# Reordering the start and the seventh pair of a fused routed-attention and SwiGLU kernel

## The chip, the cores and the metric

The kernel runs on one core of a Trainium2 chip. The metric is the device time of one execution in microseconds (us). The kernel before takes 367.86 us (median of 3 runs, 367.55 to 368.01).

## The reference

```python
# routed attention: B=4, H=8, S=768, D=64, 16 centroids for each head
q_assign = argmax(q_n @ c_n.T);  k_assign = argmax(k_n @ c_n.T)      # normalised rows
scores = scale * q @ k.T, -1e9 where q_assign != k_assign
attn = softmax(scores) @ v
# feed-forward on x = attn, as (3072, 512); d_ff = 1536
xn = x / rms(x) * rms_g
out = (silu(xn @ w_gate) * (xn @ w_val)) @ w_out
```

## The kernel before

Heads go in pairs; there are 16 pairs, `pi` 0 to 15, called the first to the sixteenth here. Each pair is prepared: q and k are transposed on TensorE (four pieces, T0 to T3), copied out of PSUM, multiplied with the centroids (`sp`), and the argmax becomes a one-hot matrix, which 16 extra rows of the score operand (`aug`) receive by DMA. So the routing mask comes out of the score matmul itself.

```python
on_dve = (g % 2 == 0 if pi == 0 else g > 1 if pi == 1 else pi < 6 or g % 2)
if on_dve:
    nc.vector.tensor_copy(dst, tp)          # VectorE (DVE)
else:
    nc.scalar.copy(dst, tp)                 # ScalarE (ACT)
# ... cut
def place():                                # one-hot rows into aug, four DMAs of 24 KB
    # ... cut
    eng = nc.sync
    if pi == 0:
        eng = nc.gpsimd if side else nc.scalar
    eng.dma_start(out=aug[st][a][D:KA, side, :].rearrange("c (r n) -> c r n", r=2),
                  in_=ohT[r:r + 2 * NC, :])
```

A main loop of 288 steps does one score chunk of 512 columns for each step (nine steps are one head, a slot). Up to step 96 three chunks share a wide PSUM tile (`scw`) and one exponential. From step 96 on, pieces of the feed-forward (gp, vp, dp) are woven in. All else is hung on steps with `at(step, fn)`; functions of one step run in the order in which they were hung there.

```python
# ... cut: first pair prepared, T0 to T3 and casts of the second
keep_warm(8)                                # dummy matmuls
for i in (SP, ARG1, ARG2, PLACE, CASTV):
    p1[i]()
first.close()
late["wide"] = wide.enter_context(tc.tile_pool(name="ps_wide", bufs=2, space=PSUM))
load_pair(3)
at(4, lambda: load_pair(4))
# ... cut
for pi in range(2, B * NP):
    base = 2 * NCH * (pi - 2) + {2: 4, 3: 1, 6: 6}.get(pi, 0)
    steps = (0, 2, 4, 6, 7, 9, 10, 12, 12, 10) if pi < 7 else (0, 1, 3, 4, 5, 8, 9, 11, 11, 9)
    for fn, step in zip(prep_parts(pi), steps):     # T0 T1 T2 T3 CAST SP ARG1 ARG2 PLACE CASTV
        at(base + step, fn)
# ... cut: weight loads
for b in range(B):                          # RMS work of the four batches
    steps = (9, 9, 10, 10, 11, 12, 13, 15, 17, 19, 20, 22, 24, 26)
    for fn, step in zip(rms_parts(b), steps):
        at(H * NCH * (b + 1) + step, fn)
```

The RMS part of a batch is: sums of squares on ScalarE and VectorE, their inverse root on GpSimd (`ir`), three normalised tiles `xn` on VectorE, and a transposing DMA (`xnT`) that feeds gp and vp; all this twice.

The softmax here doesn't subtract the row's maximum and nothing guards it: scores larger than these inputs give would overflow.

## Time and profile before

| | before |
|---|---|
| median time | 367.86 us |
| span of the profiled run | 364.7 us |
| TensorE (PE) busy | 340.2 us, 93% |
| VectorE, ScalarE busy | 222.0 and 228.0 us |
| mean granted clock | 0.985 |
| first wide score (scw) starts | 16.30 us |
| first feed-forward matmul (gp) starts | 78.81 us |

How to read the views: a page cuts the span into 40 equal slices (numbered from 0 here), and a digit is the busy share of a slice in tenths; the PEclk row is the clock that TensorE was granted, in tenths of full speed. "L287" is line 287 of the kernel, and `out<-in` names what an instruction writes and reads.

TensorE is the bound from about 91 us on. The prediction shows the lines for that, for the waits before it, and for the stretch of half clock at 67 to 77 us.

### The profile page before, as it was taken

To read this page: it belongs to the slowest core of one execution; us is meant where nothing else is said; L and a number is where in the kernel's file an instruction comes from. 1 tells how busy PE (TensorE), PEld (TensorE's weight loads), DVE (VectorE), ACT (ScalarE), POOL (GpSimd) and SP (SyncE) were. 2 spreads that over 40 slices of the span, in tenths; PEclk is the share of its full clock that TensorE was granted. 3 is DMA by queue.
4 is the path that set the end of the run, shared out by engine and by line. 5 is a ranking of instruction groups with operands and counts; after the bars stand their busy time and mean duration, and the time that the engine had idled before them with its cause. 6 is when DMAs were issued, how large, how long until landed. Compare 5 with 4: busy or idle time off the path is not lost.

```text
span 364.7 us, 7453 instructions
## 1 busy us (share of the span) xinstructions
PE 340.2 (93%) x2930; PEld 204.5 (56%) x2930; DVE 222.0 (61%) x443; ACT 228.0 (63%) x395; POOL 85.8 (24%) x119
## 2 busy tenths in 40 slices
PE   7878997688999999999999999999999979999996
PEld 4446665355666665656565665656666635555542
DVE  4766663667666648695665658695544586555540
ACT  3487888656787776867676767767777343232321
POOL 2554551762414041321204041320000011000000
PEclk9999999679999999999999999999999999999999
DMA  7449499289992310735051001431000013100012
GB/s 242 160 136 291 158 217 209 62 112 113 281 221 103 113 58 25 192 75 168 0 164 38 12 31 36 49 78 38 29 2 31 30 51 86 38 31 29 31 58 86
DMA packets 38242, 35.38 MB, mean 97 GB/s; under 512 B 15072, under 2 KB 35008, under 8 KB 38208
## 3 DMA queue, kind: packets, MB, share of 16 engines
q1 hardware_dynamic: 32080, 30.06, 27.8%
q0 software_dynamic: 5888, 4.77, 9.4%
q8 instruction: 23, 0.38, 0.4%
q10 hardware_dynamic: 240, 0.08, 0.1%
q14 instruction: 11, 0.09, 0.1%
HBM read 28.61 MB, written 6.29 MB: 96 GB/s over the span
## 4 chain that ended last, share of the span: by engine, by line
PE 75%; DVE 13%; ACT 5%; DMA 3%; issue 2%; POOL 1%; ACTq 0%; DVEq 0%
PE dp L401 15%; PE vp L372 15%; PE gp L372 15%; PE sc L287 9%; PE acc L301 7%; PE tp L193 6%; PE scw L287 4%; DVE xn L343 3%; PE sp L229 3%; DMA q_in<-in_q_dram 3%; ACT pT L290 2%; DVE gvT L387 1%; ACT jk L326 1%; DVE oh L244 1%; DVE qk L197 1%
## 5 line engine op out<-in xcount | busy, mean ns | idle before, releaser
L290 ACT ACTIVATE pT<-sc 128x512 bf16<-128x512 f32 x192 | 113.3, 597 | 54.7 <-PE sc L287 53.6
L381 DVE SCALAR_TENSOR_TENSOR uu<-th,gp 128x384 f32<-128x384 f32 x96 | 53.0, 553 | 72.9 <-ACT th L377 72.6
L372 PE MATMUL vp<-xnT,wv 128*128 128x384 bf16 x384 | 78.1, 325 | 2.6 <-DVE gvT L387 2.3
L372 PE MATMUL gp<-xnT,wg 128*128 128x384 bf16 x384 | 78.1, 325 | 1.2 <-DVE uu L381 1.0
L401 PE MATMUL dp<-wo,gvT 128*128 128x512 bf16 x288 | 76.0, 378 | 2.9 <-ACT ob L407 1.5
L377 ACT ACTIVATE th<-gp 128x384 f32<-128x384 f32 x96 | 47.1, 491 | 47.9 <-PE gp L372 44.9
L216 POOL CAST aug<-qk 64x768 bf16<-64x768 f32 x60 | 52.1, 868 | 103.8 <-DVE qk L197 100.6
L301 PEld LDWEIGHTS <-pT 128*128 128x128 bf16 x1152 | 58.5, 98 | 29.1 <-issue 3.4
L287 PE MATMUL sc<-aug 80*128 80x512 bf16 (+1 forms) x256 | 72.9, 326 | 0.0
L301 PE MATMUL acc<-vbf,pT 128*128 128x65 bf16 x1152 | 64.3, 195 | 0.2 <-DVE x L311 0.2
L387 DVE TENSOR_TENSOR gvT<-uu,vp 128x384 bf16<-128x384 f32 x96 | 52.6, 548 | 6.5 <-PE vp L372 1.4
L372 PEld LDWEIGHTS <-wg 128*128 128x128 bf16 x384 | 37.2, 97 | 30.2 <-issue 2.3
L290 ACT ACTIVATE pT<-scw 128x1536 bf16<-128x1536 f32 x32 | 45.0, 1452 | 14.4 <-PE scw L287 14.2
L372 PEld LDWEIGHTS <-wv 128*128 128x128 bf16 x384 | 37.0, 97 | 22.3 <-issue 4.2
L401 PEld LDWEIGHTS <-gvT 128*128 128x128 bf16 x288 | 27.9, 97 | 29.1 <-issue 4.4
L287 PEld LDWEIGHTS <-aug 80*128 80x128 bf16 x384 | 34.0, 98 | 17.7 <-POOL vbf L221 4.4
L197 DVE COPY qk<-tp 128x384 f32<-128x384 f32 x40 | 22.1, 554 | 25.6 <-PE tp L193 25.6
L287 PE MATMUL scw<-aug 80*128 80x512 bf16 (+1 forms) x128 | 27.2, 337 | 1.9 <-DVE tr L236 0.7
L334 POOL TENSOR_SCALAR ir<-ss 128x3 f32<-128x3 f32 x8 | 1.6, 196 | 97.8 <-ACT jk L326 97.8
L343 DVE SCALAR_TENSOR_TENSOR xn<-x,ir,g_b 128x512 bf16<-128x512 bf16 x24 | 20.5, 863 | 5.5 <-POOL ir L335 5.4
L193 PE MATMUL tp<-ident_f,k_in 128*128 128x128 f32 x96 | 17.7, 296 | 5.3 <-ACT qk L199 4.3
L193 PE MATMUL tp<-ident_f,q_in 128*128 128x128 f32 x96 | 17.8, 298 | 3.0 <-DMA q_in<-in_q_dram 2.0
(54 smaller groups left out, 204.2 us busy)
## 6 DMA issues: line engine op xcount, KB each, us to landing
q_in<-in_q_dram SPq DMA_DIRECT2D x16, 384.0 KB, 4.7
k_in<-in_k_dram SPq DMA_DIRECT2D x16, 384.0 KB, 5.1
v_in<-in_v_dram SPq DMA_DIRECT2D x16, 384.0 KB, 5.7
out_dram<-ob SPq DMA_DIRECT2D x24, 256.0 KB, 2.0
wg<-in_moe_w_gate_dram POOLq DMA_DIRECT2D x4, 384.0 KB, 5.4
wv<-in_moe_w_val_dram POOLq DMA_DIRECT2D x4, 384.0 KB, 6.7
wo<-in_moe_w_out_dram POOLq DMA_DIRECT2D x4, 384.0 KB, 7.2
aug<-ohT SPq DMA_DIRECT2D x60, 24.0 KB, 1.9
```

The costliest lines, as they stand in the source:

```text
L193: nc.tensor.transpose(tp[:, i * P:(i + 1) * P], src[:, a, i * P:(i + 1) * P], ident_f)
L197: nc.vector.tensor_copy(dst, tp)
L216: nc.gpsimd.tensor_copy(aug[st][a][0:D, :, par * HS:(par + 1) * HS], qk32[0][par * D:(par + 1) * D, 2 * a:2 * a + 2, :])
L287: nc.tensor.matmul(sc[:, o:o + n], lhsT=ag[:, 1, kc * P:(kc + 1) * P], rhs=ag[:, 0, qo:qo + n], start=True, stop=True)
L290: nc.scalar.activation(pts[slot][:, j * CH:(j + nch) * CH], sc[:, :nch * CH], ACT.Exp, scale=scale)
L301: nc.tensor.matmul(acc[:, TORD[g], :], lhsT=pts[slot][:, kc * S + g * P:kc * S + (g + 1) * P], rhs=vb[:, a, TORD[kc], :], start=(kc == 0), ...
L343: nc.vector.scalar_tensor_tensor(st["xn"][:, tl, :], x_t[b][:, t, :], st["ir"][:, tl:tl + 1], g_b, op0=ALU.mult, op1=ALU.mult)
L372: nc.tensor.matmul(pt[:, :HS], lhsT=w[:, dc, fc * P:(fc + 1) * P], rhs=xnT[b, m][:, :, dc, :], start=(dc == 0), stop=(dc == DC - 1))
L377: nc.scalar.activation(th, pt[:, :HS], ACT.Tanh, scale=0.5)
L381: nc.vector.scalar_tensor_tensor(uu, th, 1.0, pt[:, :HS], op0=ALU.add, op1=ALU.mult)
L387: nc.vector.tensor_tensor(gvT[half][:, fc, :], uu, pt[:, :HS], op=ALU.mult)
L401: nc.tensor.matmul(dp, lhsT=gvT[hf][:, f, tl * P:(tl + 1) * P], rhs=wo[:, f, :], start=(f == 0), stop=(f == FC - 1))
```

## The change

Its intent: let the first scores start before the second pair's argmax, bring the fourth pair's inputs early, and prepare the seventh pair with VectorE copies and ahead of the RMS work, so that its copies don't stand behind exponentials.

```diff
-            on_dve = (g % 2 == 0 if pi == 0 else g > 1 if pi == 1 else pi < 6 or g % 2)
+            on_dve = (g % 2 == 0 if pi == 0 else g > 0 if pi == 1 else pi < 7 or g % 2)
     keep_warm(8)
-    for i in (SP, ARG1, ARG2, PLACE, CASTV):
-        p1[i]()
     first.close()
     late["wide"] = wide.enter_context(tc.tile_pool(name="ps_wide", bufs=2, space=PSUM))
     load_pair(3)
+    for i, step in ((SP, 0), (ARG1, 0), (ARG2, 1), (PLACE, 1), (CASTV, 1)):
+        at(step, p1[i])
     ... cut
+    for b in range(B):
+        steps = (9, 9, 10, 10, 11, 12, 13, 15, 17, 19, 20, 22, 24, 26)
+        for fn, step in zip(rms_parts(b), steps):
+            at(H * NCH * (b + 1) + step, fn)
     for pi in range(2, B * NP):
-        base = 2 * NCH * (pi - 2) + {2: 4, 3: 1, 6: 6}.get(pi, 0)
+        base = 2 * NCH * (pi - 2) + {2: 3, 3: 1, 7: 4}.get(pi, 0)
     ... cut: the same RMS loop removed from behind the weight loads
```

More of the change, by code (lines that the diff above doesn't have):

```diff
@@ L468 @@
         at(step, lambda i=i: w_load(i))
-    for b in range(B):
-        steps = (9, 9, 10, 10, 11, 12, 13, 15, 17, 19, 20, 22, 24, 26)
-        for fn, step in zip(rms_parts(b), steps):
-            at(H * NCH * (b + 1) + step, fn)
     def extras(step):
```

## The prediction

> **What bounds the kernel now.** I read the page first, to see whether one engine carries the span.
>
> ```profile
> span 364.7 us, 7453 instructions
> PE 340.2 (93%) x2930; PEld 204.5 (56%) x2930; DVE 222.0 (61%) x443; ACT 228.0 (63%) x395; POOL 85.8 (24%) x119
> PE   7878997688999999999999999999999979999996
> PEclk9999999679999999999999999999999999999999
> ```
>
> TensorE is the bound over most of the span: from slice 10 on (after about 91 us) it is nearly always at 9. The change touches only what lies before that, so no more can be won than the idle or slow time of TensorE in the first 90 us. The PEclk row has a hole in slices 7 and 8 (64 to 82 us), where TensorE also has its lowest digits. So I took the timeline of TensorE next; its columns are start, duration, group, and in brackets the idle time before it with its releaser.
>
> ```profile
> 16.30 1.46 PE L287 MATMUL scw<-aug 80*128 80x512 bf16 x8 [0.71 <-DVE tr L236]
> 27.85 0.52 PE L193 MATMUL tp<-ident_f,q_in 128*128 128x128 f32 x3 [1.29 <-DMA q_in<-in_q_dram]
> 60.99 0.55 PE L193 MATMUL tp<-ident_f,k_in 128*128 128x128 f32 x3 [1.52 <-ACT qk L199]
> 64.77 0.55 PE L193 MATMUL tp<-ident_f,k_in 128*128 128x128 f32 x3 [0.95 <-ACT qk L199]
> 68.45 1.50 PE L229 MATMUL sp<-qk,cbd 128*32 128x384 f32 x8 [1.93 <-DVE qk L197]
> 73.60 0.90 PE L193 MATMUL tp<-ident_f,k_in 128*128 128x128 f32 x3 [1.27 <-ACT qk L199]
> 78.81 0.81 PE L372 MATMUL gp<-xnT,wg 128*128 128x384 bf16 x4
> ```
>
> The reader sees the three places at which the change aims: the first scores (16.30) wait for the second pair's argmax to free PSUM; the fourth pair's transposes (27.85) wait for a load; and the seventh pair's transposes and assignment wait for PSUM copies that stand on ScalarE behind exponentials, or on VectorE behind the RMS normalization. From 68.45 the eight assignment pieces take 1.50 us instead of the 0.85 they take elsewhere. The clock explains it; I asked for stretches of 3.41 us (length, PE busy, granted clock, DMA share, GB/s):
>
> ```profile
> 12.47:15.88 3.41, 2.53 (x12) 1.00 0.20 58
> 26.12:29.53 3.41, 2.12 (x26) 1.00 0.97 347
> 63.67:67.08 3.41, 1.91 (x31) 1.00 0.31 105
> 67.08:70.49 3.41, 2.04 (x15) 0.50 0.01 2
> 70.49:73.91 3.42, 2.15 (x9) 0.50 0.64 116
> 73.91:77.32 3.41, 3.41 (x28) 0.50 1.19 133
> 77.32:80.73 3.41, 2.84 (x36) 1.00 0.81 126
> ```
>
> A stretch with 1.91 us of busy time is followed by half clock; stretches with 2.12 and more are not; full clock returns only after a stretch that was full.
>
> How much is lost: steps 78 to 96 of the program (57.93 to 78.59 us) last 20.66 us with 14.35 us of PE; a comparable 18 steps before (45.99 to 55.45) last 9.46 us. So the hole is 11.2 us wide, 3% of the span; part is real work (transposes of two pairs instead of one, RMS), and 3.8 us of it (half of the 7.6 busy at half clock) is slow clock.
>
> [...] The 0.95 and 1.52 us above are that: a 0.5 us copy behind a 1.45 us exponential. [...] one-hot pieces behind loads on SyncE's queue landed after 5.8 us (median), those on other queues after 2.0. [...] Here xn takes 1.3 us beside the GpSimd casts and 0.746 in the median.
>
> **The change part by part.**
>
> *Start, second pair.* Removed: the 0.71 us wait for the argmax before the first scores, and one ScalarE copy. The first scores then need only the first pair's one-hot pieces, whose weight load could go at 15.5 us in the profile; so 0.5 to 0.8 us earlier. But the assignment (0.8 us), which filled TensorE at 13.1 to 15.6, moves behind the first scores. TensorE is then idle from 13.2 (end of the dummy matmuls) to about 15.7. The argmax chain on VectorE (0.58+0.55+0.6+0.25+0.58, about 2.7 with gaps) starts at about 17.2 instead of 15.67, and ends at 20.0 instead of 19.1. The third pair's copies stand behind it, one PSUM buffer serves its transposes, and the instruction order now has two of these before the third wide score, where there was one. So that score moves from 18.70 to about 21.1, and ScalarE idles. By my sum the fourth exponential comes at 23.3 instead of 22.11: a loss of 1.2 us.
>
> *Fourth pair's loads.* They leave SyncE's queue at about 8 to 11 us instead of 21.89 to 23.0, ahead of the one-hot pieces, so the 1.29 us wait at 26.55 goes. With the loss above, the scores at 28.40 come at about 27.75: 0.4 to 0.65 us won, if the clock holds. If it does not (idle 2.5 us in a window leaves 0.9 busy of 3.41, far under the 1.91 that throttled), half clock from about 16 us for two or three windows doubles some 4 us of TensorE work; about half hides in its 25 to 30% idle there. That costs 2 us (estimate). I give the throttle 7 in 10. Expected sum: 0.5 - 0.7 x 2 = 0.9 us lost.
>
> *Seventh pair.* It starts six steps earlier and copies all four pieces on VectorE (0.56 each; 2 x 0.5 leave ScalarE). Its steps then repeat the pattern of the sixth pair, which cost 9.46 us per 18 steps. That removes the waits 1.52, 0.95 and 1.93 and what follows from them. But the next stage begins with gp (78.81), the first reader of the transposed RMS output[...]. So I follow that chain. By the sixth pair's pattern the exponential of step 81 ends 7.54 us after step 72: 55.45 + 7.54 = 63.0 (before: 63.74). Two Squares end at 64.3, GpSimd's ir at 65.5 (1.17; before 66.61). On VectorE two xn take 2.0, then the seventh pair's one-hot work, which now stands between them (1.5), then the third xn (0.75): 69.8, before 70.4. And SyncE now issues the four one-hot DMAs (2.5 us) ahead of the DMA transpose: from about 69.0 to 71.5. The transpose was issued at 70.42 before and landed 6.0 us later; now 71.5 + 4.6 to 6.0 = 76.1 to 77.5. So gp gains only 78.81 - 76.8 = 2.0 us, though the work before it may be done at 72.
>
> TensorE idles 4 to 5 us there, and the throttle is nearly certain: one to two windows at half clock in a stage which it bounds cost 1.7 to 3.4, say 2.4 x 0.9 = 2.2 us. Against it: VectorE is ahead by then, and 1.36 us of TensorE idle at 82 to 88 goes; the eighth pair's last two transposes move into this stage (+0.7). Sum: -2.0 + 2.2 - 1.4 + 0.7 = -0.5 us.
>
> Steady state beyond: the same work. By the working alone -0.5 + 0.9 gives 0.4 us more. I go 1.5 us below that, by choice: the throttle terms are the least sure of the sum and both push up, while the removed idle is certain.
>
> **The rivals.** *The hole closes.* If the transpose's landing does not bind (issue before the one-hot DMAs, or landing after 3.7, its smallest), the 11.2 us shrink by 6 to 8: about 360. For it: 20.66 against 9.46. Against it: the chain above, with ScalarE and VectorE at 13 us of work each in 24 steps. *Two throttles.* Start 3 us worse and three slow windows after gp: about 372. For it: the 1.91 row, and three windows once already. *Hidden anyway.* The first exponentials are bound by ScalarE, the load wait is replaced by the later third score, and gp moves by under 1 us: 367 to 368.
>
> **Range and chances.** Best sum without throttles: -0.6 - 3.6 gives 363.6; worst 372. I take 366.8, with 362.5 to 371.0. A gain over 2% (under 360.5) needs the first rival whole: 0.06. A loss over 2% (over 375.2) needs long throttles at both places: 0.03.
>
> **What would show it.** Right: no wait for q_in near 27 us; third wide score past 20 us behind a VectorE copy; PEclk under 1 near 16 to 22; no waits on ScalarE's copy at 60 to 70; gp's first matmul at 76 to 78 with idle of 3 to 5 us before it, released by xnT's DMA; half clock after it. Wrong: gp at 72 to 74, or full clock all through, would make it faster; gp at 79 or later, slower.

## More of the kernel before

A further view is needed for comparison: five stages, cut at events that both kernels have. The cuts are the first and the seventh wide score, the score of step 72, the first gp, and the first transpose of the ninth pair. Columns: stretch, its length, then busy time and instructions of PE, PE weight loads, VectorE, ScalarE and GpSimd, then granted clock, DMA share, GB/s. The kernel before:

```profile
0.00:16.30 16.30, 12.98 (x58) 6.38 (x59) 8.70 (x25) 6.14 (x12) 5.55 (x18) 1.00 0.67 225
16.30:25.74 9.44, 8.02 (x80) 4.86 (x80) 5.92 (x10) 7.13 (x6) 6.84 (x9) 1.00 0.31 88
25.74:55.45 29.71, 26.81 (x354) 18.25 (x351) 20.30 (x43) 25.62 (x19) 15.01 (x20) 1.00 0.80 222
55.45:78.81 23.36, 16.82 (x162) 11.01 (x163) 11.43 (x23) 16.09 (x21) 10.88 (x14) 0.78 0.73 134
78.81:91.48 12.67, 11.30 (x109) 6.69 (x108) 10.48 (x21) 8.57 (x17) 5.37 (x6) 1.00 0.82 102
```

## The result

The changed kernel takes 376.60 us (median of 4 runs, 375.36 to 377.79); the kernel before took 367.71 us over its 4 runs. The ratio is 1.025, with a 95% interval of 1.0206 to 1.0295. A ratio is taken over means, so it is not quite the ratio of the medians. The change makes the kernel 2.5% slower; the prediction was 366.8 us with a range up to 371.0, and it gave a loss of over 2% a chance of 0.03.

The page of the changed kernel, the lines that answer to those shown of before:

```profile
span 376.0 us, 7423 instructions
PE 342.4 (91%) x2896; PEld 206.9 (55%) x2930; DVE 222.6 (59%) x446; ACT 227.5 (61%) x392; POOL 83.7 (22%) x119
PE   7388999759999999799999997999999989999996
PEclk9758999957999999999999999899999999999999
```

The hole in the PEclk row has not closed, and a second one has come: slices 1 to 3 (9 to 38 us) have a low clock, and in slice 1 TensorE is busy for only three tenths of the time. There is a third, small dip in slice 25. The same five stages of the changed kernel:

```profile
0.00:17.85 17.85, 9.24 (x50) 4.60 (x51) 8.86 (x24) 5.66 (x11) 8.24 (x21) 0.91 0.81 272
17.85:33.37 15.52, 14.29 (x89) 7.54 (x89) 5.85 (x12) 7.41 (x6) 4.15 (x6) 0.55 0.27 83
33.37:62.80 29.43, 26.79 (x354) 18.26 (x351) 20.07 (x42) 25.61 (x19) 14.87 (x19) 1.00 0.63 168
62.80:85.13 22.33, 14.44 (x155) 9.73 (x156) 12.76 (x26) 15.82 (x19) 10.34 (x14) 0.80 0.81 150
85.13:99.10 13.97, 13.95 (x114) 8.63 (x114) 8.76 (x19) 8.46 (x17) 4.76 (x7) 0.83 0.60 137
```

Length after less length before, stage by stage: +1.55, +6.08, -0.28, -1.03, +1.30. The rest of the span (376.0 - 99.10 against 364.7 - 91.48) adds +3.68. Together 11.3 us, the difference of the two profiled runs (the profiled run of the changed kernel is its slowest). So most of the loss lies in the start (+7.35 with the third stage), a part in the far tail that I had called "the same work", and the seventh pair's part is nearly even.

What opened these stages is in TensorE's timeline (start, duration, group, idle before with its releaser):

```profile
17.85 1.46 PE L287 MATMUL scw<-aug 80*128 80x512 bf16 x4 [5.80 <-DMA aug<-ohT]
24.01 0.90 PE L193 MATMUL tp<-ident_f,k_in 128*128 128x128 f32 x3 [1.23 <-DVE qk L197]
77.83 0.51 PE L301 MATMUL acc<-vbf,pT 128*128 128x65 bf16 x6 [3.70 <-DVE x L311]
85.13 1.44 PE L372 MATMUL gp<-xnT,wg 128*128 128x384 bf16 x4 [2.21 <-DMA xnT<-xn]
```

The wait for q_in at 27 us has gone, as has the one for ScalarE's copies at 60 to 70 us. In their place the first score waits 5.80 us for the first pair's one-hot DMAs; a transpose waits for a copy behind the argmax chain; and later TensorE waits for VectorE, which is held by the RMS work, and then for the transposing DMA.

The 5.80 us have a plain origin. The DMA view of each kernel, in a window over the start, gives for an issue its size and its time to landing. Before (window 9 to 16 us):

```profile
aug<-ohT ACTq DMA_DIRECT2D x2, 24.0 KB, 2.0
aug<-ohT POOLq DMA_DIRECT2D x2, 24.0 KB, 2.0
```

After (window 12 to 18 us):

```profile
aug<-ohT ACTq DMA_DIRECT2D x2, 24.0 KB, 5.6
aug<-ohT POOLq DMA_DIRECT2D x2, 24.0 KB, 5.5
```

The pieces of 24 KB are issued at 12 to 13 us on two other queues. But the fourth pair's loads (384 KB each), which SyncE issued at 6.5 to 11.6 us, keep the DMA engines fully busy until about 15.5 us (a share of 1.02 to 1.11 in each half us from 11.0 to 15.5, and 0.28 from 16.0 to 16.5), and the pieces land only after that. From 12.0 to 15.2 us the DMA view counts packets of one queue alone, SyncE's (packets, MB, share of the engines' time):

```profile
q1 hardware_dynamic: 830, 1.20, 106.9%
```

The +1.55 us understates the delay. In this run the pieces went out 0.9 us earlier than in the profiled run of before (11.98 against 12.9), and TensorE's first transposes took 0.49 to 0.55 us for three there, against 0.84 to 0.90 in the run of before.

In TensorE's idle time of 5.80 us (12.05 to 17.85) its clock falls from 1.00 to 0.50, and it falls again in the wait of 3.70 us that ends at 77.83. Stretches of 3.41 us of the changed kernel (length, PE busy, clock, DMA share, GB/s):

```profile
11.35:14.76 3.41, 0.70 (x4) 1.00 1.06 373
14.76:18.17 3.41, 0.32 (x1) 0.50 0.44 130
18.17:21.59 3.42, 3.42 (x16) 0.50 0.00 0
21.59:25.00 3.41, 2.18 (x9) 0.50 0.02 5
25.00:28.41 3.41, 3.41 (x14) 0.50 0.37 111
28.41:31.83 3.42, 3.42 (x26) 0.50 0.81 259
72.79:76.20 3.41, 0.81 (x4) 1.00 0.30 15
76.20:79.61 3.41, 1.78 (x14) 0.50 0.77 124
```

Half clock lasts five such windows in the start (14.76 to 31.83) and four around gp (76.20 to 89.85). In this trace the windows are on one grid: 76.20 is 13 windows of 3.41 us after 31.83, and in steps of 0.2 us the clock is seen to change from 14.6 to 14.8, 31.8 to 32.0, 76.2 to 76.4 and 89.8 to 90.0.

For the tail, the waits of both kernels (engine, line, what it waited for: total us, times, longest). Before:

```profile
PE dp L401 <- DVE ob L409: 1.4, 2, 0.7
DVE xn L343 <- POOL ir L335: 5.4, 3, 3.8
```

After:

```profile
PE dp L401 <- DVE ob L409: 4.1, 2, 2.0
DVE xn L343 <- POOL ir L335: 8.2, 5, 2.0
```

The moved RMS loop covers all four batches, not only the first. In the second and the third batch, too, VectorE now takes the first xn, for which GpSimd's ir isn't ready, ahead of the one-hot work and of an output copy (ob), and TensorE's dp waits for that copy. In the trace the step from the eleventh pair's first transpose to the twelfth's takes 22.45 us (before 21.13), and the one from the fifteenth's to the sixteenth's 24.00 (before 21.10); the second contains the dip of slice 25.

### The profile page after: what moved, and what is told of

Read it like the earlier page. It is cut to its first block, busy times and chain, and to the rows that moved or that the text cites. A ratio compares the mean times of both kernels' runs of the same rounds, so it can differ in the third digit from the quotient of the medians.

```text
span 376.0 us, 7423 instructions
## 1 busy us (share of the span) xinstructions
PE 342.4 (91%) x2896; PEld 206.9 (55%) x2930; DVE 222.6 (59%) x446; ACT 227.5 (61%) x392; POOL 83.7 (22%) x119
## 4 chain that ended last, share of the span: by engine, by line
PE 80%; DVE 8%; DMA 4%; ACT 3%; issue 2%; POOL 1%; POOLq 0%; DVEq 0%; ACTq 0%
PE gp L372 16%; PE vp L372 16%; PE dp L401 15%; PE sc L287 11%; PE acc L301 8%; PE tp L193 5%; PE scw L287 5%; PE sp L229 3%; DMA xnT<-xn 2%; DVE xn L343 2%; DMA aug<-ohT 1%; ACT jk L326 1%; ACT pT L290 1%; DVE oh L244 1%; POOL ir L335 1%
## 5 line engine op out<-in xcount | busy, mean ns | idle before, releaser
L372 PE MATMUL gp<-xnT,wg 128*128 128x384 bf16 x384 | 79.0, 328 | 3.3 <-DMA xnT<-xn 2.2
L372 PE MATMUL vp<-xnT,wv 128*128 128x384 bf16 x384 | 79.4, 329 | 1.2 <-DVE gvT L387 1.1
L401 PE MATMUL dp<-wo,gvT 128*128 128x512 bf16 x255 | 71.0, 378 | 7.2 <-DVE ob L409 4.1
L216 POOL CAST aug<-qk 64x768 bf16<-64x768 f32 x60 | 50.0, 834 | 119.4 <-DVE qk L197 116.7
L287 PE MATMUL sc<-aug 80*128 80x512 bf16 (+1 forms) x256 | 74.1, 331 | 0.0
L301 PE MATMUL acc<-vbf,pT 128*128 128x65 bf16 x1152 | 65.1, 196 | 4.9 <-DVE x L311 4.7
L197 DVE COPY qk<-tp 128x384 f32<-128x384 f32 x43 | 23.6, 554 | 24.9 <-PE tp L193 24.9
L287 PE MATMUL scw<-aug 80*128 80x512 bf16 (+1 forms) x128 | 30.0, 362 | 7.5 <-DMA aug<-ohT 5.8
```

Source lines behind the costliest of these rows:

```text
L216: nc.gpsimd.tensor_copy(aug[st][a][0:D, :, par * HS:(par + 1) * HS], qk32[0][par * D:(par + 1) * D, 2 * a:2 * a + 2, :])
L287: nc.tensor.matmul(sc[:, o:o + n], lhsT=ag[:, 1, kc * P:(kc + 1) * P], rhs=ag[:, 0, qo:qo + n], start=True, stop=True)
L301: nc.tensor.matmul(acc[:, TORD[g], :], lhsT=pts[slot][:, kc * S + g * P:kc * S + (g + 1) * P], rhs=vb[:, a, TORD[kc], :], start=(kc == 0), ...
L372: nc.tensor.matmul(pt[:, :HS], lhsT=w[:, dc, fc * P:(fc + 1) * P], rhs=xnT[b, m][:, :, dc, :], start=(dc == 0), stop=(dc == DC - 1))
L401: nc.tensor.matmul(dp, lhsT=gvT[hf][:, f, tl * P:(tl + 1) * P], rhs=wo[:, f, :], start=(f == 0), stop=(f == FC - 1))
```

## The experiments

The theory: three things add up. (1) The early loads delay the first pair's one-hot pieces. (2) The idle time this opens, and that which the moved assignment opens by itself, halves the clock (0.50 from 14.76 to 31.83 us above). (3) The RMS order of the later batches costs time in each. The seventh pair's part is about even. The rivals: the assignment's move alone does it; the order of transposes does it; the tail only follows from the start.

The kernels came in three groups, each on one chip with the kernel before beside it; the runs of the kernel before had medians of 367.46 (numbers 1, 2, 4, 5), 367.12 (6 to 9) and 366.89 us (3, 10 to 12). The third group used the chip of the first, and seven of its eight runs of the kernel before are those of the first group, so its ratios rest mostly on runs taken earlier.

**1. Loads behind again.** In the changed kernel:

```diff
-    load_pair(3)
     for i, step in ((SP, 0), (ARG1, 0), (ARG2, 1), (PLACE, 1), (CASTV, 1)):
         at(step, p1[i])
+    at(1, lambda: load_pair(3))
```

> The changed kernel, but the fourth pair's loads go behind the second pair's one-hot DMAs again; the assignment stays beneath the first scores. Theory T1 (the loads put ahead delay the first pair's one-hot pieces from 2.0 to 5.6 us, the 5.8 us gap this leaves halves the clock): pieces land after 2.0 us again and the first wide score starts near 16 instead of 17.85, so at least 1.5 us are won. Rival R1 (the move of the assignment alone opens a gap of 2.5 to 3 us that is enough to halve the clock): half clock still follows the first scores, and most of the loss stays, about 373 to 376. If instead the clock stays full, T1 alone explains the start and the time is 368 to 370.

Measured: 370.93 us, ratio 1.0124 (1.0061 to 1.0187). The pieces land after 2.0 us again. TensorE's timeline:

```profile
14.55 0.82 PE L287 MATMUL scw<-aug 80*128 80x512 bf16 x4 [2.43 <-DMA aug<-ohT]
19.96 0.55 PE L193 MATMUL tp<-ident_f,k_in 128*128 128x128 f32 x3 [2.56 <-DVE qk L197]
```

The first score starts 3.3 us earlier than in the changed kernel, and by the ratios 1.26% (1.025 less 1.0124, 4.6 us) is won. Half clock still follows the second gap, though only for one window (20.6 to 24.0 us; mean clock 0.87 from the first to the seventh score). So the loads are over half of the start's loss, and R1 has a share in what stays.

**2. Dummies in the gap.** In the changed kernel `keep_warm(8)` becomes `keep_warm(32)`.

> The changed kernel with 32 instead of 8 dummy matmuls ahead of the first scores, enough for the gap of 5.8 us at 216 ns each. If half clock is what costs in the start (6.1 of 7.4 us by the comparison of the traces), the first wide score still starts at 17.8 to 18, the clock is full, and first to seventh wide score takes 9.5 to 11 us instead of 15.5: total 370 to 372. Rival: the order of instructions (third score behind two transposes behind the argmax chain) costs by itself; then that stretch stays over 13 us and the total is over 374.

Measured: 374.09 us, ratio 1.0179 (1.0133 to 1.0225). That is the rival's expectation, if barely (over 374, stretch over 13 us), though not yet its reason. The 32 dummies take 7.07 us, and the first score starts at 17.37 at full clock. But T1 of the third pair then waits 2.00 us for VectorE, the clock falls to 0.50 at about 22 us all the same, and first to seventh score takes 13.6 us (17.37 to 30.98) against 15.5. Filling one gap leaves the next.

**3. Fill and old transpose order.** As the last, and `{2: 3, ...}` becomes `{2: 4, ...}`.

> The changed kernel with 32 dummies (as in a4_fill) and the third pair's transposes one step later, so that the third wide score stands behind one of them instead of two. If the order is what opened the second gap in a4_fill (2.0 us behind a VectorE copy, then half clock from 22 to 29 us), first to seventh score takes 10 to 11.5 us instead of 13.6 and the total is 371 to 373 instead of 374.1. Rival: the gap only moves by a score and the clock falls all the same; then no gain.

Measured: 374.99 us, ratio 1.0220 (1.0168 to 1.0272). The rival holds for the time: no gain. In the trace the third score is free (20.42; 22.93 in number 2), first to seventh takes 12.4 us, but a 1.36 us gap stays and the clock is half from 24.8 to 28.2 us. My expectation of 10 to 11.5 us was a miss.

**4. The start undone.** The changed kernel with the start of before (the second pair's copies, assignment and loads, and the third pair's `base`, put back).

> The changed kernel with the start of the kernel before (second pair's assignment before the scores, fourth pair's loads behind its one-hot DMAs); the seventh pair's preparation and the RMS order stay as changed. If the losses of the parts add up as the traces have them (-1.0 to gp, +1.3 after it, +1.3 at the second RMS batch, +1 to +3 at the third), the total is 368.5 to 371. Rival: the part is a gain in itself and the losses in it come from the late start; then it is at or below 366.

Measured: 368.12 us, ratio 1.0025 (0.9977 to 1.0073), just below the range expected. gp comes at 77.39 (before 78.81), and the two later batches lose 2.8 and 1.3 us in this trace. By the ratios the start is 2.25% (1.025 less 1.0025), about 8.3 us.

**5. The start alone.** The kernel before with the start of the changed one.

> The kernel before with the start of the changed kernel alone. Traces: +1.55 to the first score, +6.08 to the seventh, -0.3 after: total 374 to 376. Rival (the start's delay is swallowed by the slow stretch at 60 to 78 us, which waits on other things): under 371.

Measured: 372.07 us, ratio 1.0156 (1.0074 to 1.0238), from runs of 369.08 and 369.56, then 374.82 (marked slow, yet within the median) and 374.59 us. The three fast runs alone have a mean of 371.08 us, 1.0 to 1.2% above the kernel before in this group (mean 366.85, or 367.27 without its fastest run); the ratio is higher than they give. Either way this is between the expectation and the rival's, or close to the rival's. The profiled run is one of the short ones: 17.29 us to the first score, half clock only to about 22 us.

**6. The loads alone.** The cleanest of all: in the kernel before, `load_pair(3)` moves ahead of the second pair's `SP ... PLACE`. Only SyncE's order differs.

> The kernel before, with only the fourth pair's three loads issued ahead of the second pair's one-hot DMAs; no other engine's order changes. T1: the first pair's one-hot pieces take 5 us and more to land instead of 2.0, the first wide score starts at 17.3 or later instead of 16.3, TensorE's gap halves the clock, and in spite of the 1.29 us wait that goes, the total is 370 to 374. Rival (the loads are harmless, the moved assignment does the harm): the pieces land in 2 to 3 us and the total is 365 to 367.

Measured: 371.10 us, ratio 1.0108 (1.0053 to 1.0164). The pieces take 6.2 and 5.9 us to land, and:

```profile
18.76 2.74 PE L287 MATMUL scw<-aug 80*128 80x512 bf16 x8 [3.71 <-DMA aug<-ohT]
```

The loads are not harmless; they cost 4.0 us (1.08% of 367.1) with no assignment moved. Half clock from 17.2 to 24.0 us is in this trace as well.

**7. Later batches' RMS back.** In the changed kernel the moved loop runs over `range(1)`, and a loop over `range(1, B)` stands behind the weight loads as before.

> The changed kernel, with the RMS work of the second to fourth batch behind the attention work of the same step again (as before); the first batch's stays ahead. Theory T2: putting RMS ahead in every batch makes VectorE wait for GpSimd's ir (1.7 us) before one-hot and output work, and TensorE's dp waits 2.0 us instead of 0.7; that costs 1.3 us in each of two batches, 2.9 where half clock follows. So 2.6 to 5 us less than the changed kernel's 376.6: 371.5 to 374. Rival: the later batches' loss comes from the shifted phase of the start; then nothing is won.

Measured: 372.56 us, ratio 1.0145 (1.0096 to 1.0194): 1.05% or 3.9 us won. The two steps between pairs are 21.14 and 21.11 us again, so this loss doesn't follow from the start.

**8. Later batches' RMS ahead, alone.** The kernel before with only that.

> The kernel before, with only the RMS work of the second to fourth batch ahead of the attention work of the same step. T2: 2.6 to 5 us slower than before, 370 to 372.5, with the waits of dp at 2.0. Rival: under 368.5.

Measured: 371.10 us, ratio 1.0114 (1.0067 to 1.0161): 4.2 us slower. The waits say where:

```profile
PE dp L401 <- DVE ob L409: 4.0, 2, 2.0
```

**9. Both undone.** Number 4 with the loop of number 7.

> Both losing parts undone: start as before, later batches' RMS as before; what stays is the seventh and eighth pair's earlier preparation with VectorE copies and the first batch's RMS order. If the run with the start undone (368.1) loses 2.6 to 4 us only by the later batches, this is 364 to 366, a little faster than before. Rival: the part is worth nothing, 367 to 368.

Measured: 365.22 us, ratio 0.9961 (0.9913 to 1.0009). So the seventh pair's part alone is even to slightly faster. (Of the two pairs named, only the seventh is prepared earlier; `7: 4` puts the eighth four steps later.) Its trace shows why it is no more: gp waits 2.36 us for xnT, and the transpose is issued at 70.63, right behind four one-hot DMAs from 68.04. SyncE and TensorE in its timeline (the second of the two transposes merged in one line is a later one):

```profile
68.04 2.50 SPq L260 DMA_DIRECT2D aug<-ohT  x4
70.63 12.12 SPq L346 DMA_TRANSPOSE xnT<-xn  x2
69.40 0.51 PE L301 MATMUL acc<-vbf,pT 128*128 128x65 bf16 x6 [3.71 <-DVE x L311]
76.79 0.81 PE L372 MATMUL gp<-xnT,wg 128*128 128x384 bf16 x4 [2.36 <-DMA xnT<-xn]
```

**10. One-hot work first.** Number 9, and for the seventh pair ARG2 and PLACE come with ARG1:

```diff
-        steps = (0, 2, 4, 6, 7, 9, 10, 12, 12, 10) if pi < 7 else ...
+        steps = (0, 2, 4, 6, 7, 9, 10, 10, 10, 10) if pi == 6 else \
+                (0, 2, 4, 6, 7, 9, 10, 12, 12, 10) if pi < 7 else ...
```

> Both losing parts undone (365.2 in its run), and the seventh pair's one-hot work and its DMAs now come right after its argmax, in the time in which VectorE waits 2.0 us for GpSimd's ir, so that nothing stands between the three xn and the one-hot DMAs are issued before the transpose is ready. If the chain of RMS, one-hot DMAs and transpose sets gp (as the prediction had it), the transpose is issued about 3 us earlier after step 72, the 3.7 us wait for the eighth slot's x shrinks by over 1 us, gp comes about 19 to 20 us after step 72's score instead of 22.4, and the total is 361.5 to 363.5. Rival: gp is set by something else or lands later with the shifted loads; then within 1 us of 365.

Measured: 361.54 us (360.08 to 362.05, 6 runs), ratio 0.9832 (0.9796 to 0.9867). It beats both kernels, and is in the range expected. SyncE and TensorE in its timeline:

```profile
65.55 2.60 SPq L260 DMA_DIRECT2D aug<-ohT  x4
68.65 11.09 SPq L346 DMA_TRANSPOSE xnT<-xn  x2
69.37 0.51 PE L301 MATMUL acc<-vbf,pT 128*128 128x65 bf16 x6 [2.34 <-DVE x L311]
74.26 1.30 PE L372 MATMUL gp<-xnT,wg 128*128 128x384 bf16 x4
```

The one-hot DMAs are done when xn is, so the transpose no longer queues behind them. Step 72's score starts at 55.71, gp at 74.26: 18.55 us, against 22.42 in number 9, 22.33 in the changed kernel and 23.36 before. gp has no wait any more.

**11. Assignment beneath, on top of that.** Number 10 with the second pair's assignment beneath the first scores, the loads behind, and the third pair's transposes in the old order. The second pair's copy that the change moved from ScalarE to VectorE is moved here too.

> c1 with the second pair's assignment beneath the first scores, but the fourth pair's loads behind and the third pair's transposes in the old order (only one ahead of the third wide score). If the moved assignment is worth something by itself, the first wide score comes 0.5 to 1 us earlier and the total is 0.5 to 1 us under c1. If the gap ahead of the first scores (2.4 us in the run with the loads behind) and the later argmax chain eat that, it is equal to c1 or up to 3 us slower where the clock falls.

Measured: 365.32 us, ratio 0.9923 (0.9862 to 0.9983), so 3.3 us (0.0091 of 366.9) slower than number 10. So the moved assignment, with the copy that went with it, is a loss by itself. In its trace the pieces land after 2.0 us, the first score waits 1.97 us for them, and the clock is half from 16.8 to 27.1 us; first to seventh score takes 13.9 us (15.41 to 29.28) against 9.43 (16.69 to 26.12) in number 10. One run of the six had the clock at 0.991 instead of 0.970 to 0.977, and took 361.29, as fast as number 10; so the loss seems to be that of the clock, but one run is no proof.

**12. Early loads on another queue.** Number 10 with the fourth pair's loads issued from ScalarE's queue, after the first pair's one-hot DMAs.

> c1 with the fourth pair's loads issued from ScalarE's queue between its last copy and its first exponential, after the first pair's one-hot DMAs have been issued: early loads without standing ahead of the pieces. Pieces should land in 2 to 3 us, the first score at most 0.5 us later, any wait for q_in near 26 us gone: 0 to 1.3 us under c1. If the loads reach the pieces still in flight, the first score is late by over 1 us and it is slower than c1.

Measured: 361.34 us, ratio 0.9848 (0.9794 to 0.9903), the same as number 10. The pieces took 3.4 us (median, in a window from 12 to 18 us); no gain is shown.

## Why the prediction was wrong

What failed, by its own steps:

- *"The first scores then need only the first pair's one-hot pieces, whose weight load could go at 15.5 us in the profile; so 0.5 to 0.8 us earlier."* The pieces' landing was taken from before and put beside loads that had been moved onto them. It went from 2.0 to 5.6 us, the score came 1.55 us later, and the gap was 5.80 us, not the 2.5 that entered the sum. Numbers 1 and 6 show it from both sides: 4.6 and 4.0 us. I had compared the 2.0 us of the pieces on other queues with the 5.8 us of those behind loads on SyncE's queue, and assumed that loads on one queue don't hold up pieces on another; no trace had shown that. Those pieces had almost nothing beside them: from 12.8 to 14.1 us the loads' queue moved 28 packets, and after that none until they were through.
- *"half clock from about 16 us for two or three windows ... costs 2 us (estimate). I give the throttle 7 in 10."* Half clock came (0.50 from 14.76 us on), and the size was wrong: it was five windows, and first to seventh score took 6.08 us longer; number 2 shows that not all of it was the first gap. In the sum the start was to lose 0.9 us; in the traces it lost 7.35.
- *"The change touches only what lies before that"* and *"Steady state beyond: the same work."* False. The RMS loop was moved for all batches, as the diff says (`range(B)`). Numbers 7 and 8: 3.9 and 4.2 us.
- *"A stretch with 1.91 us of busy time is followed by half clock; stretches with 2.12 and more are not; full clock returns only after a stretch that was full."* True of the lines shown, but not a threshold: the last section has stretches of 1.64 and 1.89 us that were not followed by half clock, and one of 2.77 us that brought full clock back.
- A small misreading: the 0.95 us wait at 64.77 was for a copy behind an exponential and a sum of squares (0.62 us, then 0.19), not behind an exponential alone.

What held:

- The order of the third pair's transposes: a wait for a VectorE copy (1.23 us; 2.56 in number 1) ahead of a late third score. What it costs by itself stays open: number 3 undid it in a kernel that was slow for the other reason, and won nothing.
- The waits for q_in and for ScalarE's copies went.
- gp is held by xnT behind the one-hot DMAs (2.21 us of wait), wins little (1.03 us to gp against the 2.0 of the prediction), and is followed by half clock (+1.30 us in the next stage; the prediction's terms there, 2.2 - 1.4 + 0.7, give +1.5). Number 10, which takes these DMAs and the one-hot work off the chain together, wins 1.3% over number 9 (0.9961 less 0.9832; the two ran on different chips) and brings gp 3.9 us closer to step 72; so the chain is what held gp. Which of the two moves did more is not shown. What had been missed is that xn also holds back the eighth slot's x on VectorE (3.70 us of TensorE's idle).

The parts by ratio: start 2.25% when taken out (number 4; loads 1.1 to 1.26%, assignment with its copy 0.9%), but only 1.0 to 1.6% when put in alone (number 5), later batches 1.05 to 1.1%, seventh pair -0.4%. Start, tail and seventh pair add to 2.9 to 3.0% with number 4, and to 1.7 to 2.3% with number 5, against 2.5 measured. The intervals are about half a per cent each, so the size of the start's share stays open within these bounds.

The rival named "two throttles" (about 372) was the nearest, with a mechanism that held; it lacked the delayed pieces and the tail.

## What to carry to other kernels

When a transfer is moved earlier, price it against every small transfer that is in flight then, on other queues too: here loads on SyncE's queue went with a delay of 3.6 us (2.0 to 5.6) to pieces of 24 KB on two others, and that undid all that an early load of 1.2 MB could win. A loop that hangs work on steps moves for all its iterations; compare the instruction order of the whole program, not of the part that was meant. Put work that is ready into the time in which the next item waits: in number 9 VectorE waits 2.00 us for ir ahead of xn; number 10 puts the one-hot work there, waits 0.48 us, and wins 1.7% over the kernel before.

## What the runs leave open

- What halves the clock and what brings it back. Half clock followed a window of 3.41 us with 1.91 us busy (kernel before, 63.67 to 67.08) and windows with 0.70 and 0.81 (changed kernel). It did not follow one with 1.64 (kernel before, 295.76 to 299.17) nor one with 1.89 (number 8, 57.01 to 60.42), so busy time as the profile counts it does not decide alone. The same holds for the way back: two full windows at half clock in the changed kernel (18.17 to 21.59, 25.00 to 28.41) were followed by half clock again, and one with 2.77 us busy in number 1 (78.61 to 82.02) by full clock. What decides stays open.
- Where the scatter of one kernel comes from. The kernel before ran in 364.34 us at a mean clock of 0.995 and in 368.81 at 0.971, on one chip and in one group of runs. Whether it depends on where the windows fall was not tested.
- What a small transfer loses beside large ones on another queue. Here 24 KB took 2.0 us with almost nothing beside them, 5.5 to 6.2 us beside loads of 384 KB (experiment 6 and the changed kernel), and 3.4 us where the loads were issued after them (experiment 12). In the changed kernel 830 packets of the loads' queue moved from 12.0 to 15.2 us, and none of the pieces issued from 12.0 us on. Why is not shown.
